# Attention and two feed-forward layers on one core: SBUF rooms taken in a fixed order, with moving and stationary operands 64 bytes apart modulo 256

## The chip, the cores and the metric

One core of a Trainium2 chip runs the whole kernel in one launch. The metric is the device time of one execution in microseconds; the time of the kernel before is the median of three runs.

## The reference

Sparse attention over 4 batches of 8 heads, 576 positions of 64 (four heads local, four strided by 32), gives x of 2304 x 512. Then two feed-forward layers without a residual follow, each from 512 to 2048 and back:

```python
def _moe_ref(x, w_in, w_out):
    h = x @ w_in
    g = np.where(h >= 1, h, np.where(h <= -1, 0.0, (h + 1) ** 2 / 4))
    return (g @ w_out).astype(np.float32)

def _moe2_ref(x, w_in, w_out, s, b):
    h = x @ w_in
    r = np.maximum(h, 0.0)
    g = s * (r * r) + b
    return (g @ w_out).astype(np.float32)
```

The output is `_moe2_ref(_moe_ref(x))`, all in float32. About nine tenths of TensorE's time are the four products with `w_in` and `w_out`.

## The kernel before

**Products.** Every float32 operand of the four big products is split into a high and a low part of type fp32r, and a product is three matmuls: high by high, high by low, low by high. Tokens go in 9 blocks of 256 (`g` from 0 to 8 for the first feed-forward layer, 9 to 17 for the second, called the first and the second half here); the 2048 hidden columns go in 8 pairs of two tiles of 128 (`p`). The step of one block and one pair has two layers:

- layer one (`layer1`, L838): the moving tile is a part of x (`xh` or `xl`, 256 columns), the stationary tile 128 columns of `w_in`; 2 x 4 x 3 = 24 matmuls go into the PSUM tile h;
- layer two of the first half (`layer2`, L993): the moving tile is a part of the activated g, the stationary one 128 columns of `w_out`; 24 matmuls into y;
- layer two of the second half (`layer2_fast`, L906): seven products of half-size blocks in place of eight (sums and differences of blocks are formed first, by `combine` at L881 for the activations and `w_combine` at L714 for the weights); here the *weights* move (256 columns) and g's parts (`gh`, `gl`) stand; 7 x 3 = 21 matmuls into y.

Each matmul loads its own stationary tile first; in the profile this is an LDWEIGHTS on PEld, which runs beside the matmul before it. Layer two of a pair comes `LAG = 2` pairs after layer one, so the rows of h and y alternate. Attention's small matmuls stand between them in about the first 345 us, and idle matmuls of a tile of zeros (`u`, both operands) fill gaps in the first 45 us.

**Order of work.** All operations are recorded by `Order` (L120), put into one order for all engines by `Order.issue` (L272) from prices and due times that are written in the kernel, and emitted there (L386, the line of nearly every row in the profile). Addresses play no part in that order, and neither the order nor any price is touched by the change.

**Rooms in SBUF.** A room is a tag with a shape; tiles of one tag use it one after the other. `Order.real` (L161) asks the pool for a room when the first tile of the tag is emitted, and rooms lie one behind the other in the order in which they were asked for, each start rounded up to 32 bytes. In the kernel before that is the order of first use. Most rooms are multiples of 256 bytes long, so the start modulo 256 changes only behind a room that is not: `half` (4 bytes), `narrow` (620 bytes) and `sbt` (8 bytes). This leaves, in the kernel before:

| rooms | start modulo 256 |
|---|---|
| xh, xl (moving in layer one) | 32 |
| w tiles of 4 KB, named w(f)_(0: w_in, 1: w_out), f from 0 to 15 | 32, but for these: 64 for w9_1 and w3_1; 128 for w7_1 and w9_0; 160 for w8_0, w7_0, w15_0, w15_1 |
| g (moving in layer two of the first half, gh in the second) | 64 |
| as, raw0, raw1 (gl in the second half) | 128, 160, 160 |
| xr1 (its four quarters hold weights in the second half) | 128 |
| u (zeros, both operands of the idle matmuls) | 128 |

All slices of these rooms that a big matmul reads start at a multiple of 256 bytes from the room's start, so the start modulo 256 is that of every slice. Pair p of the first half reads w tiles 2p and 2p + 1, the first with its 12 matmuls ahead of the other's in layer one, and in turns of three matmuls in layer two. In the stretch from 340 to 400 us of the profile, layer one has pairs 4 to 7 of block 5, 0 to 3 of block 6 and 0, 1 and on of block 7, and layer two runs two pairs behind: its pieces are pairs 2, 3, 4, ... of block 5 and then 0, 1, 2, 3 of block 6. The second half's weights take rooms that the first half's left free.

Of the kernel before, what the change touches and what calls it, by code (L numbers as in the profile page):

```python
# [20 lines left out]
P = 128  # L21
# [5 lines left out]
NF = DFF // P  # L27
# [89 lines left out]
    )  # L117


class Order:  # L120


# [30 lines left out]
    def bank(self, pool, choices, name, kind):  # L153


        t = self.tile(pool, [P, 512], F32, f"bank_{kind}", len(self.choices) + 1, name)
        self.choices[t.tensor.name] = choices
        self.uses[t.tensor.name] = []
        return t

    def real(self, x):  # L161

        if not isinstance(x, bass.AP) or x.tensor.name not in self.place:
            return x
        (tag, _), pool, shape, dtype, bufs, name = self.place[x.tensor.name]
        if x.tensor.name not in self.tiles:
            if self.in_psum(x):
                tag, bufs = self.taken[x.tensor.name], 1
            self.tiles[x.tensor.name] = pool.tile(shape, dtype, tag=tag, bufs=bufs, name=name)
        t = self.tiles[x.tensor.name]  # L170
        v = bass.AP(tensor=t.tensor, offset=x.offset, ap=[list(d) for d in x.ap])
        return v if x.dtype == dtype else v.bitcast(x.dtype)
# [217 lines left out]
def attention_moe_moe(ctx, tc, q, k, v, w1_in, w1_out, w2_in, w2_out, s_in, b_in, consts, out):  # L390
    nc = Order(tc.nc)
# [4 lines left out]
    ident = nc.tile(sb, [P, P], F32, "ident")  # L396
    narrow = nc.tile(sb, [P, N_CONST], BF16, "narrow")
    mask_l, mask_s, ident_b = narrow[:, :N_MASK_L], narrow[:, N_MASK_L:N_MASK_L + N_MASK_S], narrow[:, N_MASK_L + N_MASK_S:]
    sbt = nc.tile(sb, [P, 2], F32, "sbt")
# [287 lines left out]
    wc = {}  # L687
# [189 lines left out]
    def turn(i, rooms, name):  # L877
        n_room[i] += 1
        return rooms[n_room[i] % len(rooms)](name)

    def combine(g, p, u, h, gt):  # L881

        (a21, a11, a22, a12), (h21, h11, h22, h12) = [[x[:, i * P:(i + 1) * P] for i in range(4)] for x in (u, h)]
        s4 = turn(0, (main["qk"][0], main["v"][0]), f"s{g}_{p}")[:, :4 * P]
        s1, s2, s3, s4_ = [s4[:, i * P:(i + 1) * P] for i in range(4)]
        gh = gt.rearrange("p x n -> p (x n)")[:, :7 * P]
        if (g, p) == LAST:
            gl = xs[g, 1][1].rearrange("p x n -> p (x n)")[:, :7 * P]
        else:
            gl = turn(1, (*main["raw"], main["s"]), f"gl{g}_{p}")[:, :7 * P].bitcast(F32R)  # L890

        def split(x, c, eng=nc.gpsimd):
            nc.scalar.activation(out=gh[:, c], in_=x, func=AF.Copy)
            eng.tensor_tensor(out=gl[:, c], in0=x, in1=gh[:, c].bitcast(F32), op=ALU.subtract)

        nc.vector.tensor_tensor(out=s1, in0=h21, in1=a22, op=ALU.add)
        nc.vector.tensor_tensor(out=s2, in0=s1, in1=h11, op=ALU.subtract)
        nc.vector.tensor_tensor(out=s3, in0=h11, in1=a21, op=ALU.subtract)
        nc.vector.tensor_tensor(out=s4_, in0=h12, in1=s2, op=ALU.subtract)
        split(u[:, P:], slice(0, 3 * P))  # L900
        split(s4, slice(3 * P, 7 * P), nc.vector if g == LAST[0] and p >= NP - 2 else nc.gpsimd)
        gs[g, p] = gh, gl
# [48 lines left out]
    def last_two(g, p0, part):  # L951
        y, o = ys.pop(g), [turn(2, (main["qk"][1], main["v"][1]), f"o{g}_{p0}_{i}")[:, :DM] for i in range(2)]
        (c21, c22), (c11, c12), (p21, p22), (p11, p12), (m1, m6), (m2, m5), (m4, m7), (m3, _) = [
            (x[:, :HM], x[:, HM:]) for x in (*o, part[:, 0], part[:, 1], *y)
        ]
        pairs = [(p, gs.pop((g, p))) for p in (NP - 2, NP - 1)]

        def multiply(n, p, x):
            a, b = PRODUCTS[n]
            o, c, w = y[n // 2][:, n % 2 * HM:(n % 2 + 1) * HM], slice(a * P, a * P + P), wt[1, p][b]  # L960
            for i, j in ((0, 0), (0, 1), (1, 0)):
                nc.tensor.matmul(o, x[i][:, c], w[:, j], start=False, stop=p == NP - 1 and i == 1, skip_group_check=True)

        def leave(i, j, c, queue):
            r0 = (g - NBLK) * N + i * P
            queue.dma_start(out=out[r0:r0 + P, j * HM:(j + 1) * HM], in_=c)

        nc.in_line = True
        for i, n in ((0, 0), (0, 1), (0, 2), (0, 3), (1, 0), (1, 1), (1, 2), (1, 3), (0, 4), (0, 5), (1, 4), (1, 5), (0, 6), (1, 6)):
            multiply(n, *pairs[i])  # L970
        nc.in_line = False
        add = dict(op=ALU.add)
        nc.scalar.activation(out=c11, in_=m1, func=AF.Copy)
        nc.gpsimd.tensor_tensor(out=p11, in0=c11, in1=p11, **add)
        nc.vector.tensor_tensor(out=c21, in0=m6, in1=c11, **add)
        nc.gpsimd.tensor_tensor(out=p21, in0=c21, in1=p21, **add)
        nc.vector.tensor_tensor(out=c22, in0=m5, in1=c21, **add)
        nc.gpsimd.tensor_tensor(out=p22, in0=c22, in1=p22, **add)
        nc.vector.tensor_tensor(out=c11, in0=m2, in1=p11, **add)
        leave(1, 0, c11, nc.sync)  # L980
        nc.vector.tensor_tensor(out=p12, in0=c22, in1=p12, **add)
        nc.scalar.activation(out=p11, in_=m7, func=AF.Copy)
        nc.vector.tensor_tensor(out=p21, in0=m7, in1=p21, **add)
        nc.gpsimd.tensor_tensor(out=c22, in0=p11, in1=p22, **add)
        leave(0, 1, c22, nc.sync)
        nc.vector.tensor_tensor(out=c21, in0=p21, in1=m4, op=ALU.subtract)
        leave(0, 0, c21, nc.scalar)
        nc.vector.tensor_tensor(out=c12, in0=m3, in1=p12, **add)
        leave(1, 1, c12, nc.scalar)
# [36 lines left out]
    half = nc.tile(sb, [P, 1], F32, "half")  # L1026

    def room(tag, width):
# [4 lines left out]
        p=[room("qp0", 5 * P), room("qp1", S)], v=[room("v0", 9 * D), room("v1", 9 * D)],  # L1033
# [64 lines left out]
    with tc.manual_schedule():  # L1098
        nc.now = -100
        nc.sync.dma_start(out=ident, in_=consts[:, N_MASK_L + N_MASK_S:])  # L1100
        wide = x_room("wide", N_CONST)[:, 0]
        nc.sync.dma_start(out=wide[:, :N_CONST], in_=consts)
        nc.gpsimd.memset(half, 0.5)
        nc.vector.tensor_copy(narrow, wide[:, :N_CONST])

        nc.now = -1000
        zeros = nc.tile(sb, [P, 2 * N], F32R, "u", bufs=U_BUFS)
        nc.gpsimd.memset(zeros.bitcast(F32), 0.0)
        idle = nc.bank(ps, ("y1",), "idle", "y")
        nc.tensor.matmul(idle[:, :256], zeros[:, :P], zeros[:, :256], start=True, stop=True)  # L1110
        nc.fill(idle[:, :256], zeros[:, :P], zeros[:, :256])
        nc.now = -100
        for i, t in enumerate(STARTS):
            b, pair = divmod(i, 4)
            plan(Unit(b, FIRST_PAIRS[pair], borrowed(MEMORY[i]) if i in MEMORY else main, i < QUICK, i < NATURAL), t)
        for f in range(NF):
            plan_w(f)
        at(todo[0][0], pump)

        run(-1)  # L1120
        nc.sync.dma_start(out=sbt[:, 0:1], in_=bass.AP(tensor=s_in.tensor, offset=s_in.offset, ap=[[0, P], [1, 1]]))
        nc.sync.dma_start(out=sbt[:, 1:2], in_=bass.AP(tensor=b_in.tensor, offset=b_in.offset, ap=[[0, P], [1, 1]]))
        nc.now = -15
        x_split(0)
        nc.now = -2
        x_split(1)
        slot, behind = 0, []
        for n, (g, p0, p1) in enumerate(PASSES):

            order = []  # L1130
            for p in range(p0, p1):
                order.append((1, g, p0, p1, p))
                behind.append((2, g, p0, p1, p))
                if len(behind) > LAG:
                    order.append(behind.pop(0))
            nxt = PASSES[n + 1][0] if n + 1 < len(PASSES) else g
            if n + 1 == len(PASSES):
                order.insert(-2, order.pop(-2))
            for i, (layer, b, *pp, p) in enumerate(order):
                run(slot)  # L1140
                if slot == 0:
                    nc.fill()
                if layer == 1:
                    activate(b, p, layer1(b, p))
                else:
                    second(b, p, *pp)
                if i == p1 - p0 + 1 and nxt not in xs:
                    x_split(nxt)
                elif i == p1 - p0 + 1 and n + 1 == len(PASSES):
                    part = last_part(g, p0)  # L1150
                slot += 1
        nc.now += 1
        last_two(g, p0, part)
        nc.issue()


# [24 lines left out]
```

## Time and profile before

| | before |
|---|---|
| median of 3 runs | 897.74 us (897.33 to 898.22) |
| the profiled execution | 898.65 us |
| its span, first to last instruction | 896.9 us |
| mean granted TensorE clock | 0.998 of full speed |
| TensorE matmuls, weight loads | 8937 each, busy 99% and 98% |
| VectorE, ScalarE, GpSimd | busy 54%, 55%, 47% |
| DMA | 103.38 MB, 115 GB/s |

The profiled execution is one run with the profiler on; durations come from it. It is 0.9 us over the median. "h <- xh,w" names a matmul's result, its moving and its stationary tile, without buffer numbers.

### The profile page before, as it was taken

What the parts mean: (1) busy time and instruction counts of PE and PEld (TensorE: products, weight loads), DVE (VectorE), ACT (ScalarE), POOL (GpSimd) and SP (SyncE); (2) the same over time, 40 slices, a digit from 0 to 9 for tenths busy, and PEclk for the clock granted to TensorE, in tenths of its full rate; (3) what the DMA queues carried; (4) which work ended last, traced back from release to release, by engine and by line L of the source; (5) the groups of instructions that cost most, each with busy time, mean ns of one, the idle gap of its engine ahead of it and who ended that gap; (6) DMA issues with size and microseconds to landing.
All of it is one profiled execution on the core that took longest, in us unless ns stands there. A gap on an engine that the chain in (4) does not pass through costs nothing.

```text
span 896.9 us, 22117 instructions
## 1 busy us (share of the span) xinstructions
PE 888.9 (99%) x8937; PEld 877.1 (98%) x8937; DVE 483.4 (54%) x1006; ACT 489.9 (55%) x1086; POOL 423.6 (47%) x363
## 2 busy tenths in 40 slices
PE   9999999999999999999999999999999999999998
PEld 8999999999999999999999999999999999999998
DVE  3678764344334432333675778545457854454545
ACT  2577776444434442333644676656667655555554
POOL 6266562211121121223454578767755855544554
PEclk9999999999999999999999999999999999999999
DMA  9898523223312311003626633424334332222211
GB/s 176 235 284 276 191 75 98 66 47 78 66 21 64 73 66 48 25 24 102 212 88 211 206 125 133 150 94 147 137 104 180 118 117 94 96 96 94 95 48 48
DMA packets 125534, 103.38 MB, mean 115 GB/s; under 512 B 86688, under 2 KB 103840, under 8 KB 125432
## 3 DMA queue, kind: packets, MB, share of 16 engines
q1 hardware_dynamic: 122008, 100.52, 37.6%
q8 instruction: 70, 1.15, 0.5%
q10 hardware_dynamic: 2656, 0.85, 0.5%
q0 software_dynamic: 768, 0.60, 0.4%
q14 instruction: 32, 0.26, 0.1%
HBM read 73.63 MB, written 28.31 MB: 114 GB/s over the span
## 4 chain that ended last, share of the span: by engine, by line
PE 96%; ACT 1%; DVE 1%; POOL 1%; issue 0%; DMA 0%; SPq 0%; DVEq 0%; ACTq 0%; POOLq 0%
PE h L386 45%; PE y L386 42%; PE s L386 3%; PE idle L386 3%; PE o L386 2%; PE p L386 1%; PE t L386 1%; ACT u L386 0%; DVE wc L386 0%; ACT w L386 0%; DMA raw<-in_q_dram 0%; ACT g L386 0%; POOL g L386 0%; DVE u L386 0%; POOL xl L386 0%
## 5 line engine op out<-in xcount | busy, mean ns | idle before, releaser
L386 PE MATMUL h<-xh,w 128*128 128x256 f32 x2304 | 442.2, 284 | 0.5 <-ACT xh L386 0.3
L386 PEld LDWEIGHTS h<-xh,w 128*128 128x128 f32 x2304 | 368.4, 191 | 2.0 <-issue 0.6
L386 PE MATMUL h<-xl,w 128*128 128x256 f32 x1152 | 326.1, 283 | 0.0
L386 PE MATMUL y<-g,w 128*128 128x256 f32 x1728 | 222.1, 281 | 0.1
L386 PEld LDWEIGHTS h<-xl,w 128*128 128x128 f32 x1152 | 219.6, 191 | 0.1
L386 PEld LDWEIGHTS y<-g,w 128*128 128x128 f32 x1728 | 210.3, 188 | 1.0 <-DVE o L386 0.3
L386 POOL TENSOR_TENSOR g<-u,g 128x512 fp32r<-128x512 f32 x72 | 96.6, 1342 | 240.2 <-ACT g L386 158.8
L386 PE MATMUL y<-w,g 128*128 128x256 f32 x852 | 155.7, 281 | 0.0
L386 ACT ACTIVATE u<-h 128x512 f32<-128x512 f32 x144 | 85.8, 597 | 108.6 <-PE h L386 68.4
L386 DVE TENSOR_SCALAR u<-h 128x512 f32<-128x512 f32 x72 | 49.6, 690 | 152.3 <-PE h L386 152.2
L386 PEld LDWEIGHTS y<-w,g 128*128 128x128 f32 x852 | 130.9, 188 | 0.0
L386 ACT ACTIVATE u<-u,half 128x512 f32<-128x512 f32 x72 | 52.0, 723 | 126.0 <-DVE u L386 125.9
L386 POOL TENSOR_TENSOR gl<-u,g 128x384 fp32r<-128x384 f32 x71 | 74.1, 1044 | 97.3 <-ACT g L386 90.0
L386 PE MATMUL y<-w,gl 128*128 128x256 f32 x426 | 119.0, 281 | 0.0
L386 DVE TENSOR_SCALAR h<-h,sbt 128x512 f32<-128x512 f32 x72 | 58.8, 816 | 110.8 <-ACT h L386 110.7
L386 POOL TENSOR_TENSOR gl<-s,g 128x512 fp32r<-128x512 f32 x70 | 91.8, 1311 | 33.1 <-ACT g L386 30.1
L386 ACT ACTIVATE g<-u 128x512 fp32r<-128x512 f32 (+1 forms) x143 | 82.5, 578 | 32.9 <-DVE u L386 25.2
L386 POOL TENSOR_TENSOR w<-wc,w 128x512 fp32r<-128x512 f32 x56 | 77.1, 1379 | 39.4 <-ACT w L386 36.2
L386 PEld LDWEIGHTS y<-w,gl 128*128 128x128 f32 x426 | 80.1, 188 | 0.0
L386 DVE TENSOR_TENSOR u<-h,u 128x512 f32<-128x512 f32 x72 | 49.4, 686 | 28.8 <-ACT u L386 28.6
L386 ACT ACTIVATE g<-s 128x512 fp32r<-128x512 f32 x71 | 44.6, 629 | 20.8 <-DVE s L386 20.8
L386 DVE TENSOR_TENSOR s<-h,u 128x128 f32<-128x128 f32 x144 | 35.1, 284 | 32.6 <-ACT u L386 32.4
(112 smaller groups left out, 970.1 us busy)
## 6 DMA issues: line engine op xcount, KB each, us to landing
wr<-in_moe_w_in_dram SPq DMA_DIRECT2D x32, 512.0 KB
wr<-in_moe_w_out_dram SPq DMA_DIRECT2D x32, 512.0 KB
x<-o SPq DMA_DIRECT2D x36, 256.0 KB
scratch<-x SPq DMA_DIRECT2D x18, 512.0 KB
y<-o SPq DMA_DIRECT2D x22, 256.0 KB
scratch<-y SPq DMA_DIRECT2D x11, 512.0 KB
xhd<-xh SPq DMA_DIRECT2D x8, 512.0 KB
xld<-xl SPq DMA_DIRECT2D x8, 512.0 KB
```

Of the source, the lines that this page charges most:

```text
L386: getattr(getattr(self.nc, engine), op)(*args, **kw)
```

## The change

A list `HOMES` names every room of SBUF; `Order.settle` asks the pool for them in that order, after everything has been recorded and before `issue` emits the first instruction (L1154 before). `half` and `sbt`, each rounded up to 32 bytes, stand ahead of as, raw0, raw1 and narrow in the list, and narrow (620 bytes, 640 with rounding) ahead of xh, xl and g. `combine` puts gh 32 elements (128 bytes) further into its room.

```diff
--- before.py
+++ after.py
@@ -117,6 +117,13 @@
     )
 
 
+G_SHIFT = 32
+HOMES = (
+    "ident", "u", *(f"w{f}_{x}" for f in range(NF) for x in range(2)), "xr0", "xr1", "v0", "v1", "mx", "sm", "qp0", "qp1", "wc",
+    "half", "sbt", "as", "raw0", "raw1", "narrow", "xh", "xl", "g",
+)
+
+
 class Order:
 
 
@@ -157,6 +164,13 @@
         self.choices[t.tensor.name] = choices
         self.uses[t.tensor.name] = []
         return t
+
+    def settle(self, tags):
+
+        for tag in tags:
+            name = f"{tag}_0"
+            pool, shape, dtype, bufs, title = self.place[name][1:]
+            self.tiles[name] = pool.tile(shape, dtype, tag=tag, bufs=bufs, name=title)
 
     def real(self, x):
 
@@ -883,7 +897,7 @@
         (a21, a11, a22, a12), (h21, h11, h22, h12) = [[x[:, i * P:(i + 1) * P] for i in range(4)] for x in (u, h)]
         s4 = turn(0, (main["qk"][0], main["v"][0]), f"s{g}_{p}")[:, :4 * P]
         s1, s2, s3, s4_ = [s4[:, i * P:(i + 1) * P] for i in range(4)]
-        gh = gt.rearrange("p x n -> p (x n)")[:, :7 * P]
+        gh = gt.rearrange("p x n -> p (x n)")[:, G_SHIFT:G_SHIFT + 7 * P]
         if (g, p) == LAST:
             gl = xs[g, 1][1].rearrange("p x n -> p (x n)")[:, :7 * P]
         else:
@@ -1151,6 +1165,7 @@
                 slot += 1
         nc.now += 1
         last_two(g, p0, part)
+        nc.settle(HOMES)
         nc.issue()
```

The five engines' instructions and waits stand in the same order before and after. What is different is where the operands lie. After the change all w rooms, xr0, xr1, v, qp, wc and u start at 128 modulo 256, as, raw0 and raw1 at 192, xh, xl and g at 64, and gh, 128 bytes into g, at 192. The pairs of a matmul's moving tile and the next matmul's stationary tile, for the big products that follow each other directly, then stand as follows (difference: stationary minus moving, modulo 256; numbers of pairs):

| | before | after |
|---|---|---|
| layer one | 2310 at 0, 297 at 32, 203 at 96, 619 at 128 | 3342 at 64, 87 at 128 (switches to layer two of the second half) |
| layer two, first half | 1265 at 224, 215 at 0, 116 at 96, 105 at 64 | 1701 at 64 |
| layer two, second half | 754 at 32, 278 at 128, 157 at 96, 141 at 0, 139 at 192, 42 at others | 1418 at 64, 86 at 0 (switches to layer one), 7 at 192 (the last block) |

## Rows read from the trace of the kernel before

**Rows 1.** The page, part 1: busy us of each engine (share of the span) xinstructions.

```profile
PE 888.9 (99%) x8937; PEld 877.1 (98%) x8937; DVE 483.4 (54%) x1006; ACT 489.9 (55%) x1086; POOL 423.6 (47%) x363
```

**Rows 2.** The page, part 4: the chain that ended last, by engine and by line.

```profile
PE 96%; ACT 1%; DVE 1%; POOL 1%; issue 0%; DMA 0%; SPq 0%; DVEq 0%; ACTq 0%; POOLq 0%
PE h L386 45%; PE y L386 42%; PE s L386 3%; PE idle L386 3%; PE o L386 2%; PE p L386 1%; PE t L386 1%; ACT u L386 0%; DVE wc L386 0%; ACT w L386 0%; DMA raw<-in_q_dram 0%; ACT g L386 0%; POOL g L386 0%; DVE u L386 0%; POOL xl L386 0%
```

**Rows 3.** Groups by shape on PE: out<-in, rows*columns, shapes xcount, busy us, mean ns, idle.

```profile
L386 PE MATMUL h<-xh,w 128*128 128x256 f32 x2304 | 442.2, 284 | 0.5 <-ACT xh L386 0.3 <-DVE s L386 0.2
L386 PE MATMUL h<-xl,w 128*128 128x256 f32 x1152 | 326.1, 283 | 0.0
L386 PE MATMUL y<-g,w 128*128 128x256 f32 x1728 | 222.1, 281 | 0.1
L386 PE MATMUL y<-w,g 128*128 128x256 f32 x852 | 155.7, 281 | 0.0
L386 PE MATMUL y<-w,gl 128*128 128x256 f32 x426 | 119.0, 281 | 0.0
...
L386 PE MATMUL y<-halves,g 128*128 128x256 f32 x106 | 21.8, 281 | 0.9 <-ACT g L386 0.8
...
L386 PE MATMUL y<-halves,last_l 128*128 128x256 f32 x1 | 0.3, 279 | 0.0
```

**Rows 4.** Stretches: length, then PE, PEld, DVE, ACT, POOL busy (x), clock, DMA share, GB/s.

```profile
350.00:400.00 50.00, 50.00 (x425) 50.00 (x424) 15.46 (x24) 15.27 (x24) 11.35 (x9) 1.00 0.06 22
500.00:550.00 50.00, 49.75 (x417) 49.33 (x416) 42.69 (x88) 38.90 (x75) 35.40 (x28) 1.00 0.47 165
```

**Rows 5.** The chain, 340 to 400 us: start, us until the next piece, engine, tile, matmuls.

```profile
340.89 2.83 PE h L386 x24
343.73 2.83 PE y L386 x24
346.56 2.86 PE h L386 x24
349.42 2.81 PE y L386 x24
352.23 2.88 PE h L386 x24
...
392.05 2.87 PE h L386 x24
```

**Rows 6.** The chain, 590 to 640 us, second half of the work.

```profile
592.25 2.84 PE h L386 x24
595.09 2.47 PE y L386 x21
597.56 2.86 PE h L386 x24
600.42 2.48 PE y L386 x21
```

**Rows 7.** Groups by shape on PEld (weight loads), 352.3 to 354.9 us.

```profile
L386 PEld LDWEIGHTS h<-xh,w 128*128 128x128 f32 x15 | 2.4, 191 | 0.0
```

**Rows 8.** Groups by shape on PEld, 341 to 343.5 us.

```profile
L386 PEld LDWEIGHTS h<-xh,w 128*128 128x128 f32 x15 | 2.3, 188 | 0.0
```

**Rows 9.** Timeline of PE, 35 to 36 us: start, first start to last end, matmuls.

```profile
34.72 1.48 PE L386 MATMUL idle<-u 128*128 128x256 f32 x11
```

**Rows 10.** Timeline of PE, 395.98 to 396.06 us.

```profile
395.71 0.62 PE L386 MATMUL y<-g,w 128*128 128x256 f32 x4
```

**Rows 11.** Timeline of PE, 396.68 to 396.77 us.

```profile
396.40 0.64 PE L386 MATMUL y<-g,w 128*128 128x256 f32 x4
```

**Rows 12.** Stretches, matmuls into h alone: length, PE busy (x), clock, DMA share, GB/s.

```profile
0.00:50.00 50.00, 4.87 (x25) 0.98 1.04 221
50.00:100.00 50.00, 27.32 (x195) 0.99 0.93 285
```

**Rows 13.** Stretches, matmuls into y alone.

```profile
50.00:100.00 50.00, 20.60 (x157) 0.99 0.93 285
```

## The prediction

> **What bounds the kernel now.** First the page's busy times: TensorE is busy 99% of the 896.9 us span, its weight loads 98%, no other engine over 55% [rows 1]. Then the chain of work that ended last: 96% of it is TensorE, nearly all matmuls into h (layer one) and y (layer two) [rows 2]. So the time is a count of matmuls times their spacing. The groups by shape give the count [rows 3]: 2304 + 1152 for layer one, 1728 for layer two of the first half, 852 + 426 and eight smaller rows of 234 together for layer two of the second half. That is 3456 + 1728 + 1512 = 6696 matmuls of 256 columns, each with a weight load of its own. The mean of 281 to 284 ns in those rows is the length of one matmul in the pipeline, not the spacing; the reader should take the spacing from the chain, whose pieces follow each other start to start.
>
> In a stretch where TensorE never waits and the granted clock is 1.00 (2.4 GHz) [rows 4], the chain alternates between 24 matmuls into h and 24 into y [rows 5]. From the h piece at 340.89 to the h piece at 392.05 us lie nine pieces of each kind, 18 x 24 = 432 matmuls: 51.16 us / 432 = 118.4 ns. The y pieces of the second half have 21 matmuls in 2.47 or 2.48 us, 117.6 to 118.1 ns [rows 6]. 256 columns at 2.4 GHz are 106.7 ns. Some 12 ns of each spacing, 6696 x 11.8 = 79 us in all, are thus neither columns nor waits, and in that remainder lies everything this change can touch.
>
> **What the rows say about addresses.** The change alters only addresses. The question is whether the spacing hangs on (address of the stationary tile minus address of the moving tile) modulo 256, here called the difference; while one matmul streams, the weights of the next are read, so the pair is that matmul's moving tile and the next one's stationary tile. The old rooms are scattered enough to try this without a new run:
> - Difference 0, layer one, pairs whose two weight tiles both lie at 32 (10 and 11, 12 and 13): 2.86 and 2.88 us for 24 [rows 5], 119.2 and 120.0 ns. The idle matmuls, whose two operands are one tile, so also difference 0, show the same in another part: (1.48 - 0.28) / 10 = 120 ns [rows 9].
> - Difference 128 and 96, the same layer and the same moving rooms (weight tiles 8 and 9, at 340.89): 2.83 us [rows 5], 117.9 ns.
> - Difference 224, layer two (weight tiles 4 and 5, at 343.73): 2.83 us, 117.9 ns. Half 224 and half 64 (tiles 6 and 7, at 349.42): 2.81 us, 117.1 ns.
>
> The weight loads agree: 191 ns where the difference is 0 [rows 7], 188 ns at 96 and 128 in the same layer 11 us earlier [rows 8]. It is therefore not the layer, nor what other engines do: DMA share in this stretch is 0.06 and ACT and DVE are busy a third of it [rows 4].
>
> Difference 64 is rare before the change (weight tile 7 of layer two only, three matmuls at a time). Within one piece it takes two values. Four matmuls from 395.71 last 0.62 us; less the 0.28 of the last, three spacings of 113.3 ns [rows 10]. Four from 396.40, same tile and same difference, last 0.64: three of 120.0 ns [rows 11]. So the spacing depends on more than the pair at hand: on how far the two streams had fallen behind each other before. Difference 0 shows what a long stretch does: over ten idle matmuls the mean is 120 ns, the highest value of all, as if the streams settled at a fixed distance and stayed there. I take it that a long stretch of difference 64 settles too, and choose 113.3 for it, because no other difference in these rows comes that low and 120 is where difference 0 already sits. That is a choice between two values that the rows show, and the rivals price the other.
>
> **The change, part by part.**
> 1. *Order of work*: the instructions of all five engines stand in the same order, with the same waits. Nothing is added, removed or moved past a queue: 0 us.
> 2. *Differences*: with the new rooms layer one, layer two of the first half and the products of the second half all have 64, except where the second half switches between layers: there the last moving tile and the first stationary tile differ by 0 or 128, at 86 and 87 places. Price before: 6696 x 118.4 = 792.8 us (the second half's y pieces are a little under that, its h pieces at 2.84 to 2.86 a little over [rows 5, 6]). After, from below: 6696 x 113.3 = 758.7, a gain of 34.1 us. From above there are two bounds: the mean over both values of tile 7, which is the mixed piece's 117.1 less the 224 half's 117.9, so 2 x 117.1 - 117.9 = 116.3 ns: 778.7, a gain of 14.1; and the long value alone, 120.0: 803.5, a loss of 10.7. I take 113.3, for the reason above.
> 3. *Switches in the second half*: 173 places x three matmuls until the short spacing is back (the h piece at difference 0 is my guide only for the height, 120.0; three is an estimate) x 6.7 ns = 3.5 us given back.
> 4. *The first 100 us*: the DMA engines are full there (shares 1.04 and 0.93), so weights cannot arrive sooner. 25 + 195 matmuls into h and 157 into y [rows 12, 13] gain at most 377 x 5.1 = 1.9 us; I count it as lost to waits.
> 5. *The shift of g's part by 32 elements* (128 bytes): same writes and reads at another place in the same room, 0 us; the busy time of ACT, POOL and DVE has cover, since PE's lag of two pairs (about 11 us) stands between h and its use. If that cover is gone anywhere, it is at 500 to 550 us, where DVE is busy 42.7 and ACT 38.9 of 50 [rows 4]: 4.4% less time for the same work makes DVE 44.6 of 50 on that scale, still under PE.
> 6. *Attention's small matmuls and the tail after the last product*: their rooms move too, by no rule that a row here shows; with the idle matmuls they are about 10% of the chain [rows 2], some 90 us, and half a per cent of that is 0.4 us either way.
>
> Sum: -34.1 + 3.5 + 1.9 = -28.7 us. The profiled execution took 898.65 us (896.9 span and 1.75 around it), 0.9 over the median of 897.74, so the forecast is 897.74 - 28.7 = **869 us**.
>
> The Trainium skill speaks against the change. "TensorE: Matmul & The Clock Gate", Part 2, says that TensorE has two independent SBUF read ports and that loading the next weights takes no read bandwidth from the running matmul; "SBUF — State Buffer", in the section on the two sides, that PE's port never waits for anyone. By that rule addresses cost nothing and the sum is 0. The trace disagrees: 2.88 against 2.83 us for equal work [rows 5].
>
> **Rivals.**
> - *It settles in between* (chance 0.28). Runs of 64 keep alternating between 113 and 120 as tile 7 does: 14.1 gained, less half of items 3 and 4, 11.4: 886, with 875 to 889 as its span. For it: the alternation is what the rows show. Against it: in those rows difference 224 comes between, after the change nothing does.
> - *It settles at the long spacing* (0.10). The triple at 396.40 is the stable one. The turning point is a mean of 118.4 ns: above it the kernel is slower. At 120.0 it is 10.7 us more: 908; at 119, 902. For it: [rows 11]. Against it: no row shows 120 lasting at difference 64, and the piece as a whole is the shortest of its kind [rows 5].
> - *The address does not matter* (0.06), and the 2.83 and 2.88 come from the tiles' other properties (which banks of PSUM, what lies behind). Then 897.7. This is what the skill's rule would give. Against it: rows 7 and 8.
> - *The change doesn't do what it says*: excluded as far as it can be seen beforehand; the rooms as built have the differences given. *Another engine becomes the bound* would show first at 500 to 550 us: all of the gain of that stretch lost is 417 x 5.1 = 2.1 us, inside the range.
>
> **How the numbers follow.** Likeliest, 0.56: the short spacing, 864 (items 3 and 4 at nothing) to 874 (twice their price). With the next case it reaches to 889; 16 in 100 lie above. A spacing a little under 113.3 (0.62 is rounded: 112.0 would be 8.7 us more) takes the lower end to 858. A measurement of this kernel can tell about 0.2% (1.8 us). Faster by more: 0.56 + 0.28 = 0.84; within: 0.06; slower: 0.10.
>
> **What would show it.** Chain pieces of 24 matmuls into h and into y should both be about 2.72 us, with no difference between layers, and in 350 to 400 us over 440 matmuls should stand where 425 do. Weight loads of h should fall from 191 to 188 ns or less. PE should stay at 98% or more busy; waits of PE for ACT, DVE or DMA of several us would mean that the spacing fell and the time went elsewhere. If pieces of one kind stay at 2.86 or more while the differences are 64, the account by the difference is wrong. If they are near 2.79 and vary, the first rival holds.

## The result, and the profile after

| | before | changed |
|---|---|---|
| median, same chip (4 runs each) | 897.98 us (897.33 to 898.34) | 876.85 us (875.2 to 877.0) |
| ratio, 95% interval | | 0.9761 [0.9744, 0.9778] |
| profiled execution, its span | 898.65, 896.9 us | 876.75, 875.0 us |

The change gains 21.1 us, 2.4%; the forecast was a gain of 28.7 us, to 869. The page of the changed kernel, busy times and the chain that ended last, by engine and by line, stands against [rows 1, 2]:

```profile
PE 866.1 (99%) x8937; PEld 854.0 (98%) x8937; DVE 485.3 (55%) x1006; ACT 490.0 (56%) x1086; POOL 424.9 (49%) x363
...
PE 95%; ACT 1%; DVE 1%; DMA 1%; issue 1%; POOL 1%; POOLq 0%; DVEq 0%; ACTq 0%
```

The instruction counts are the same and no other engine was relieved: DVE, ACT and POOL are busy as long as before, PE 22.8 us less. PE is still 99% busy, so the time left the spacing of its matmuls. Stretches of the changed kernel (length, PE, PEld, DVE, ACT, POOL busy, clock, DMA share, GB/s):

```profile
350.00:400.00 50.00, 50.00 (x443) 50.00 (x443) 15.92 (x24) 15.27 (x24) 12.91 (x10) 1.00 0.06 22
500.00:550.00 50.00, 49.72 (x425) 49.31 (x424) 39.29 (x87) 37.56 (x72) 41.93 (x33) 1.00 0.38 136
```

At the same granted clock of 1.00, 443 matmuls stand where 425 did, and 425 where 417 did [rows 4]. The chain (start, us until the next piece, engine, tile, matmuls) shows where it came from. The stretch of [rows 5], which now starts 7.69 us earlier (the h piece of 340.89 is at 333.20):

```profile
333.20 2.72 PE h L400 x24
335.92 2.72 PE y L400 x24
```

All 20 pieces from 330.48 to 382.16 are 2.72 us: 113.3 ns, in both layers, whatever the weight tile. In the second half it looks different, where [rows 6] had 2.84 to 2.86 for h and 2.47, 2.48 for y:

```profile
740.92 2.74 PE h L400 x24
743.66 2.47 PE y L400 x21
746.13 2.74 PE h L400 x24
```

h is at 114.2 ns, but y still at 117.6: layer two of the second half gained nearly nothing, although its pairs stand at difference 64 like the rest. And before 305 us, where attention's small matmuls come between:

```profile
287.05 2.72 PE h L400 x24
289.77 1.64 PE s L400 x74
291.41 3.02 PE y L400 x24
294.44 2.83 PE h L400 x24
```

After the 74 small matmuls into s the same products at the same difference run at 2.83 us (117.9 ns) up to the next interruption, the small matmuls into p at 303.39 us. Worked out from the start times of all matmuls that follow each other directly: of 237 stretches of twelve spacings in the first half of the changed kernel, each begun at least eight matmuls behind an interruption, 194 have a mean of 113.3 ns (one of them 113.2), 43 one of 117.8, and none lies between. The mean spacings by part, before and after: layer one 119.2 and 114.6 (114.3 in the first half, 114.9 in the second); layer two of the first half 117.4 and 114.4; layer two of the second half 118.5 and 117.3; all together 118.6 and 115.2. The groups by shape on PE show it too (against [rows 3]; the mean is the length of one matmul, not the spacing):

```profile
L400 PE MATMUL h<-xh,w 128*128 128x256 f32 x2304 | 426.5, 279 | 1.1 <-DVE s L400 0.7 <-ACT xh L400 0.3
...
L400 PE MATMUL y<-g,w 128*128 128x256 f32 x1728 | 217.0, 279 | 0.1
L400 PE MATMUL y<-w,g 128*128 128x256 f32 x852 | 154.3, 281 | 0.0
...
L400 PE MATMUL y<-halves,g 128*128 128x256 f32 x106 | 22.1, 284 | 1.4 <-ACT g L400 1.0 <-DVE o L400 0.4
```

284 and 281 became 279 for h and the first half's y; the second half's y kept its 281. The weight loads of h between 333.2 and 335.9 us take 188 ns, where [rows 7] had 191:

```profile
L400 PEld LDWEIGHTS h<-xh,w 128*128 128x128 f32 x15 | 2.3, 188 | 0.0
```

### The profile page after: what moved, and what is told of

Read it like the earlier page. It is cut to its first block, busy times and chain, and to the rows that moved or that the text cites. A ratio compares the mean times of both kernels' runs of the same rounds, so it can differ in the third digit from the quotient of the medians.

```text
span 875.0 us, 22117 instructions
## 1 busy us (share of the span) xinstructions
PE 866.1 (99%) x8937; PEld 854.0 (98%) x8937; DVE 485.3 (55%) x1006; ACT 490.0 (56%) x1086; POOL 424.9 (49%) x363
## 4 chain that ended last, share of the span: by engine, by line
PE 95%; ACT 1%; DVE 1%; DMA 1%; issue 1%; POOL 1%; POOLq 0%; DVEq 0%; ACTq 0%
PE h L400 44%; PE y L400 41%; PE s L400 3%; PE idle L400 3%; PE o L400 2%; PE p L400 1%; PE t L400 1%; DMA wr<-in_moe_w_out_dram 1%; ACT u L400 0%; DVE wc L400 0%; ACT w L400 0%; DVE o L400 0%; DVE s L400 0%; ACT g L400 0%; POOL g L400 0%
## 5 line engine op out<-in xcount | busy, mean ns | idle before, releaser
L400 PE MATMUL h<-xh,w 128*128 128x256 f32 x2304 | 426.5, 279 | 1.1 <-DVE s L400 0.7
L400 PEld LDWEIGHTS h<-xh,w 128*128 128x128 f32 x2304 | 361.3, 189 | 2.7 <-issue 1.3
L400 PE MATMUL h<-xl,w 128*128 128x256 f32 x1152 | 320.7, 278 | 0.0
L400 PEld LDWEIGHTS h<-xl,w 128*128 128x128 f32 x1152 | 217.4, 189 | 0.1
L400 PE MATMUL y<-g,w 128*128 128x256 f32 x1728 | 217.0, 279 | 0.1
L400 PEld LDWEIGHTS y<-g,w 128*128 128x128 f32 x1728 | 205.3, 188 | 1.0 <-DVE o L400 0.3
L400 DVE TENSOR_SCALAR wc<-wr 128x512 int32<-128x512 int32 x64 | 49.5, 787 | 8.6 <-DMA wr<-in_moe_w_out_dram 6.6
```

The source lines that it names most:

```text
L400: getattr(getattr(self.nc, engine), op)(*args, **kw)
```

## The experiments

The theories, by the letters that the texts on record use. **A**: the difference alone sets the spacing of a long stretch. **B**: it is the absolute address, that operands now start at a multiple of 64 bytes. **C**: it is the fixed order, what lies beside what. **D**: a difference can have two steady spacings, and a stretch keeps one until something disturbs it. **E**: each pair's difference fixes its spacing, with no memory. **F**: the step of 128 at the entry to the second half's layer two puts it on the long spacing. **G**: those products are long of themselves. In what follows an order means the last nine names of `HOMES`; the changed kernel has half, sbt, as, raw0, raw1, narrow, xh, xl, g and `G_SHIFT` 32. The edits are shown by the names or lines that change; "..." stands for lines left out. Ratios are to the kernel before on the same chip (medians 897.85 to 898.97 us).

**1. e1_same: fixed order, difference 0 everywhere.**

```diff
-G_SHIFT = 32
+G_SHIFT = 0
-    "half", "sbt", "as", "raw0", "raw1", "narrow", "xh", "xl", "g",
+    "as", "raw0", "raw1", "xh", "xl", "g", "narrow", "half", "sbt",
```

> Fixed order of rooms, but every big room (w, x, g, as, raw) at the same start modulo 256 and gh not shifted, so that the difference (stationary minus moving, modulo 256) is 0 in all 6696 big matmuls. Theory A (the difference alone sets the spacing, and a long stretch settles at one value): 120 ns everywhere, pieces of 24 in 2.88 us and of 21 in 2.52 us, about 907 us, slower than both kernels. Theory B (what counts is that rooms start at a multiple of 64 bytes, which they still do): about 877 us. Theory C (what counts is the fixed order, which rooms are neighbours): about 877 us.

905.88 us, ratio 1.0086 [1.0061, 1.0112]: slower than before. Its chain, at 341 us and in the second half:

```profile
341.25 2.88 PE h L399 x24
344.13 2.88 PE y L399 x24
...
760.06 2.88 PE h L399 x24
762.94 2.52 PE y L399 x21
```

Every piece that nothing interrupts is at 120 ns, in both layers and halves. The rooms are in a fixed order and start at multiples of 64 bytes, as in the changed kernel, and the same instructions take 29 us more than there. A holds so far; B and C fall, and a fixed order is worth nothing by itself.

**2. e2_shift32: the changed kernel, all rooms 32 bytes further.**

```diff
-    "ident", "u",
+    "pad8", "ident", "u",
...
```

The lines left out have `settle` ask for the pad, 8 elements of 4 bytes.

> The changed kernel with a pad of 32 bytes ahead of all rooms: every address 32 bytes further, no room at a multiple of 64 any more, all differences as in the changed kernel. Theory A: no change, 876 to 878 us, pieces of 24 in 2.72 us in the first half. Theory B: the gain goes, 890 to 898 us. Theory C: 876 to 878 us.

876.06 us, ratio 0.9754 [0.9729, 0.9779]; not to be told from the changed kernel, and its chain at 331 us has the same 2.72:

```profile
333.66 2.72 PE h L402 x24
```

B falls a second time, now with the differences kept.

**3. e3_second192: 64 in layer one and the first half, 192 in the second half's layer two, 0 at all its switches.**

```diff
-G_SHIFT = 32
+G_SHIFT = 0
-    "half", "sbt", "as", "raw0", "raw1", "narrow", "xh", "xl", "g",
+    "half", "sbt", "narrow", "as", "raw0", "raw1", "xh", "xl", "g",
```

> The changed kernel, but gl's rooms and gh at 64 modulo 256 (gh not shifted, narrow ahead of as, raw0 and raw1): difference 64 in layer one and in the first half, 192 (minus 64) in layer two of the second half, and 0 at both switches of the second half. Theory A: layer one and the first half stay at 113.3 ns; layer two of the second half is at 117.3 ns in the changed kernel because the switch with difference 128 pushes it to a second, longer spacing. If 192 is as good as 64 and the switch with 0 does not push, its pieces of 21 fall from 2.46 to 2.38 us and the whole to about 869 us; if 192 has a spacing of its own near 117.5 the whole stays at 877; at 120 it is 881. Theories B and C: 877 us.

875.57 us, ratio 0.9751 [0.9728, 0.9774], the same as the changed kernel within the intervals. But the chain is another one:

```profile
742.41 2.47 PE y L399 x21
744.88 2.73 PE h L399 x24
747.62 2.38 PE y L399 x21
750.00 2.83 PE h L399 x24
752.83 2.47 PE y L399 x21
```

y takes 2.47 and 2.38 in turn, h 2.73 and 2.83 in turn. So layer two at 192 can run at 113.3, and layer one at 64 can run at 117.9. Going from h to y keeps the spacing, going from y to h changes it. That is D, and not E; A falls too, as far as it takes one spacing for each difference.

**4. e4_first192: 192 in layer one and the first half, 64 in the second half's layer two, 0 at its switches.**

```diff
-G_SHIFT = 32
+G_SHIFT = 0
-    "half", "sbt", "as", "raw0", "raw1", "narrow", "xh", "xl", "g",
+    "half", "sbt", "as", "raw0", "raw1", "xh", "xl", "g", "narrow",
```

> The mirror image: difference 192 in layer one and in the first half (x and g 64 bytes above the weights), 64 in layer two of the second half (gh not shifted), 0 at both switches of the second half. Theory A: layer two of the second half at 64 and without the switch of 128 settles at 113.3 ns, pieces of 21 in 2.38 us, 6 us gained there; layer one and the first half show what 192 is worth over long stretches: 113.3 would make it 871 us, 117.5 some 21 us more, 891, and 120 some 905. Theories B and C: 877 us.

886.56 us, ratio 0.9871 [0.9835, 0.9907]. The chain, at 340 us and in the second half:

```profile
340.12 2.83 PE h L399 x24
342.95 2.83 PE y L399 x24
...
751.40 2.40 PE y L399 x21
753.80 2.72 PE h L399 x24
756.52 2.48 PE y L399 x21
759.00 2.83 PE h L399 x24
761.82 2.39 PE y L399 x21
```

At 340 us everything is on the long spacing at 192. In the second half both layers alternate again, but now going from h to y changes the spacing and going from y to h keeps it, and the second half's y runs at 2.39 at difference 64, the very difference at which it takes 2.47 in the changed kernel. G falls: nothing in these products holds them at the long spacing.

**5. e5_homes_alone: the new order of rooms without the shift of gh.**

```diff
-G_SHIFT = 32
+G_SHIFT = 0
```

> The fixed order of rooms alone, gh not shifted: difference 64 in layer one and in the first half as in the changed kernel; in layer two of the second half 192 for the pairs that load gh and 64 for those that load gl; 0 at both switches of the second half. If layer two of the second half keeps whichever of the two spacings it comes in with (the switch with 0 did so in the mirror runs), its pieces of 21 are a mixture of 2.38 and 2.47 us and the whole is 873 to 877 us. If the mixed differences have a spacing of their own near 118, 878 us. If the shift of gh is what brings the gain: 890 us or more.

876.83 us, ratio 0.9765 [0.975, 0.978]. The second half alternates as in experiment 3 (y 2.38 and 2.50, h 2.83 and 2.73 from 744.25 us; 2.50 is 119.0 ns, somewhat over the long spacing, in pieces whose pairs stand at 64 and at 192). The shift brings nothing that can be measured: it turns "every y long, every h short" into "each in turn", with the same sum.

**6. e6_all192: 192 everywhere, the shift kept.**

```diff
-    "half", "sbt", "as", "raw0", "raw1", "narrow", "xh", "xl", "g",
+    "half", "sbt", "xh", "xl", "g", "narrow", "as", "raw0", "raw1",
```

> Difference 192 (minus 64) in all big products, with 128 and 0 at the switches of the second half, as the changed kernel has them with 64. If 192 is as good as 64 (two spacings, 113.3 and 117.8, and the way in decides which), about 877 to 888 us, and pieces of 24 in the first half are either 2.72 or 2.83 us and nothing between. If only 64 is good: 893 us or more, all pieces at 2.82 or over.

889.63 us, ratio 0.9909 [0.9889, 0.993]. The chain, in the first half and in the second:

```profile
219.35 1.47 PE s L399 x46
220.82 2.92 PE y L399 x24
223.74 2.72 PE h L399 x24
...
744.37 2.47 PE y L399 x21
746.84 2.83 PE h L399 x24
```

Most of the first half and all of the second is on the long spacing, but after some interruptions by attention, as here behind the 46 matmuls into s, the same products at the same difference take the short one. 64 and 192 have the same two spacings; they do not have the same share of each: by the count of stretches used above, 23 of 237 are at 113.3 here and 214 at 117.8.

**7. e7_flip: one spare matmul in the changed kernel, both operands one weight tile, in a stretch at 113.3.** It adds one product whose result is not used.

```diff
+                    if (b, p) == (5, 6):
+                        t = wt[0, 2 * p + 1, 0]
+                        spare = nc.bank(ps, U_BANKS, "spare", "u")
+                        nc.tensor.matmul(spare[:, :N], t[:, 0, :P], t[:, 0, :N], start=True, stop=True)
```

> The changed kernel with one matmul more, between layer one of block 5, pair 6, and the next layer two (about 344 us): both its operands are a weight tile, so the pair behind it has difference 0, every other pair keeps its own. Its result is not used. Theory D (two steady spacings at difference 64, 113.3 and 117.8 ns, kept until something disturbs it): the one disturbance moves the first half to 117.8 ns, pieces of 24 from 2.72 to 2.83 us from there to about 490 us, and costs some 5.7 us: 882 to 883 us. Theory E (the difference of the pair alone sets each spacing, without memory): 0.12 us for the one matmul, 877.0 us.

876.18 us, ratio 0.976 [0.9742, 0.9778]. Its chain:

```profile
346.35 0.12 PE spare L400
346.46 2.74 PE y L400 x24
349.21 2.72 PE h L400 x24
```

The flip that D expected did not come. About five matmuls are disturbed (0.02 us in the piece behind), then 113.3 is back. D in this form is too simple: this one wrong pair does not change the spacing of the stretch.

**8. e8_96_160: 96 in layer one and the first half, 160 in the second half's layer two.**

```diff
-G_SHIFT = 32
+G_SHIFT = 0
-    "half", "sbt", "as", "raw0", "raw1", "narrow", "xh", "xl", "g",
+    "half", "narrow", "as", "raw0", "raw1", "xh", "xl", "g", "sbt",
```

> Difference 96 in layer one and in the first half, 160 (minus 96) in layer two of the second half, 0 at the switches. The rows of the kernel before had 118.0 ns at 96 over 12 at a time and too few at 160. If every difference but 0 settles at one of the two spacings: 113.3 gives 868, 117.8 gives 896. If 96 keeps its own 118: about 895 to 898 us, like the kernel before.

894.66 us, ratio 0.9966 [0.9953, 0.9978]. Its chain:

```profile
304.66 2.85 PE h L399 x24
...
347.23 2.81 PE y L399 x24
350.04 2.82 PE h L399 x24
...
743.19 2.52 PE y L399 x21
```

96 gives 117 to 118 ns where nothing comes between, and up to 119 behind attention's small matmuls (2.85 at 304.66) and at every other h of the second half (2.82 and 2.85 in turn); 160 gives 120.0. Neither shows 113.3 over a long stretch.

**9. e9_bridge: one spare matmul at each entry to the second half's layer two,** both operands a weight tile, so that the two sides no longer step by 128 at once. Its results are not used.

```diff
+        t = wt[1, p]["t2"]
+        spare = nc.bank(ps, U_BANKS, "spare", "u")
+        nc.tensor.matmul(spare[:, :HM], t[:, 0, :P], t[:, 0, :HM], start=True, stop=True)
...
```

The lines left out have the spare matmul wait for what y's first one waits for.

> The changed kernel with one matmul more at each entry into layer two of the second half (72 of them; in 66 it stands right ahead of y's first): weights move and weights stand in it, so that the step from layer one has difference 64, 64 in place of 128. Its result is not used. Theory F (the step of 128 at the entry is what puts layer two of the second half on the longer spacing): most of its pieces of 21 fall from about 2.47 to 2.38 us, 4 to 6 us gained, against 72 x 0.113 = 8.2 us added: 878 to 882 us. Theory G (something in those products themselves makes 117.3 ns): pieces stay at 2.46 or more, 885 us.

883.3 us, ratio 0.9829 [0.9806, 0.9853]. Its chain:

```profile
622.77 0.12 PE spare L400
622.89 2.47 PE y L400 x21
```

y stays at 2.47 (53 of its 54 whole pieces at 2.47 or 2.48), so the spare matmuls are paid for and y gives nothing back. The 6.5 us over the changed kernel are fewer than the 8.2 that 72 of them cost; in the profiled executions most of the difference comes from around 650 us, where the changed kernel waits (see below) and this one does not. By the addresses of the rooms the spare matmul stands between h and y with 64 on both sides at 59 of the 72 places. F falls in this form.

**10. e10_first_part: the entry made 64 without a spare matmul.** The first of gh's seven parts lies 64 bytes lower than the others, so that most entries step by 64, with one pair at 0 after the first part.

```diff
-        gh = gt.rearrange("p x n -> p (x n)")[:, G_SHIFT:G_SHIFT + 7 * P]
+        gh = gt.rearrange("p x n -> p (x n)")[:, G_SHIFT - 16:G_SHIFT + 7 * P]
...
+            d = 16 * (c.start > 0)
+            h = gh[:, c.start + d:c.stop + d]
...
```

> The changed kernel with the first of gh's seven parts 64 bytes lower, so that the entry into layer two of the second half has 64 at 63 of 80 places; the price is one pair of difference 0 right behind it, and that part is written by instructions of its own on ACT and POOL. Theory F: if that pair of 0 is absorbed, as the single one in the first half was, the pieces of 21 fall to about 2.39 us and the whole to 870 to 872 us; if it sets the longer spacing as the step of 128 did, 877 us; ACT and POOL have time for the two instructions more.

876.35 us, ratio 0.9758 [0.973, 0.9785]. y is at 2.48 and h at 2.74 (from 620.25 us in its chain), as in the changed kernel:

```profile
620.25 2.48 PE y L400 x21
```

By itself this leaves it open whether the pair of 0 right behind the entry sets the long spacing, as the text above allows for. With experiment 9, which has no such pair, it is a second sign against F: the difference at the entry by itself does not decide.

**11. e11_shift_alone: the kernel before, with the shift of gh alone.**

```diff
-        gh = gt.rearrange("p x n -> p (x n)")[:, :7 * P]
+        gh = gt.rearrange("p x n -> p (x n)")[:, 32:32 + 7 * P]
```

> The other part of the change alone: the kernel before, its rooms as they were, with gh 32 elements further. The differences in layer two of the second half become 160, 128, 96 and 64 in place of 32, 128, 96 and 192, those elsewhere stay. The mirror run had 119.9 ns at a steady 160 against 118.5 at 32 before, over half of 1512 matmuls: 1 us slower, 898 to 900 us. If the shift carries a part of the gain by itself: below 895 us.

900.02 us, ratio 1.0015 [1.0004, 1.0027], some 1 us slower, as expected. Together with experiment 5: the rooms bring the whole gain.

**12. e12_three_steps: three spare matmuls in e6_all192, in a stretch on the long spacing,** with both operands a weight tile, then weight by x, then both x. Their results are not used.

```diff
+                    if (b, p) in ((5, 6), (6, 1), (7, 1)):
+                        t, x = wt[0, 2 * p + 1, 0][:, 0, :N], xs[b][0][:, 3]
+                        s, m = {5: (t, t), 6: (t, x), 7: (x, x)}[b]
+                        spare = nc.bank(ps, U_BANKS, "spare", "u")
+                        nc.tensor.matmul(spare[:, :N], s[:, :P], m, start=True, stop=True)
```

> The kernel with 192 everywhere, whose first half stands at 117.8 ns from about 341 us to its end near 490 us, with one matmul more at three places between layer one and layer two (results not used): at about 347 us with both operands a weight tile (difference 0 and 0 on the way), at 370 us with a weight tile and x (difference 192 throughout, a control), at 393 us with both operands x (0 on the way). If 113.3 and 117.8 ns are two steady spacings at one difference, a single disturbed matmul can move the stream from the one to the other: behind the first or the third the pieces of 24 go from 2.83 to 2.72 us and stay there, and the run is up to 5.4 us faster than the 889.6 us without them, although it does three matmuls more. The control changes nothing. If the long spacing belongs to this difference and stretch, or if neither disturbance moves it, all pieces stay at 2.83 and the run is 889.6 + 0.4 = 890.0 us.

892.29 us, ratio 0.9937 [0.9914, 0.996]. Its chain, around the first and the third spare matmul:

```profile
348.46 2.83 PE h L399 x24
351.29 0.13 PE spare L399
351.42 2.82 PE y L399 x24
...
391.10 0.12 PE spare L399
391.22 2.83 PE y L399 x24
```

None of the three takes the stretch off its long spacing; by the addresses of the rooms the first and the third bring one pair at 0 each. The 2.7 us over experiment 6 are more than the three matmuls (0.4 us). In the two profiled executions, 1.85 us apart, 1.5 us arise between 38 and 61 us: from 37 to 62 us the granted clock has a mean of 0.93 here, so a part of it is at 1.2 GHz, and of 1.00 in experiment 6. But the slowest of the four runs, 892.96 us, has a mean clock of 1.0, so what the rest of the 2.7 is stays open.

What the runs say of each difference over long stretches:

| difference | ns per matmul | where |
|---|---|---|
| 0 | 120.0 | e1_same, all parts |
| 64 | 113.3 or 117.8 | changed kernel; e3_second192 layer one; e4_first192 second y |
| 192 | 113.3 or 117.8 | e6_all192; e3_second192 second y; e4_first192 layer one |
| 96 | 117 to 118, up to 119 in some stretches | e8_96_160, layer one and the first half |
| 160 | 120.0 | e8_96_160, layer two of the second half |

## Why the prediction held, and where it missed

**The mechanism (the section on addresses, and item 2) was right.** The spacing hangs on the difference and not on the absolute address (e2_shift32), nor on the fixed order (e1_same), and 113.3, chosen from the three spacings of [rows 10], is a value to which a long stretch settles: pieces of 2.72, as forecast, in all 60 whole pieces of the first half behind 330 us. The price of 120.0 for difference 0, from the idle matmuls [rows 9], was also exact.

The choice of 113.3 had more behind it than [rows 10]: of the 33 undisturbed triples at 64 in layer two of the first half before, 16 have a mean of 113.3 ns or just over, and no triple at 0, 96 or 224 there is under 115.7. That it came out to the digit is in part luck, since [rows 10] are three spacings from times rounded to 0.01 us, 3 ns for each. And no row said which of the two values would last; the explanation given beside it, how far the two streams had fallen behind each other, is shown by no run.

**What failed is the assumption behind items 2 and 3, that a stretch at 64 has one value and that a switch only costs three matmuls until it is back.** 64 has two steady values. The text had seen that the spacing "depends on more than the pair at hand", and still took it that a long stretch settles to one. The higher one is not the 120.0 of [rows 11] but 117.8. The switches of the second half were priced at 3.5 us; in fact nearly every y piece of 21 stays on the long spacing from end to end (42 of 44 whole ones at 2.47). By the mean spacings that is (117.3 - 113.3) x 1501 = 6.0 us for y and (114.9 - 113.3) x 1675 = 2.7 for the second half's h, together 8.7, so 5.2 more than priced.

**A term was missing: the first half behind attention.** About a fifth of its matmuls, in stretches that begin after attention's small ones, run at the long spacing (2.83 at 294.44): (114.35 - 113.3) x 3379 directly following matmuls = 3.5 us. The step was to read 400 us of undisturbed products as if the 345 before them were the same.

**Item 4 was wrong the other way.** 1.9 us in the first 100 us were counted as lost to DMA; the same h piece at about 100 us starts 1.56 earlier than before (98.33 against 99.89), of which 0.73 stand at 10 us already, before any product, and so are not of this mechanism.

These three make 5.2 + 3.5 - 1.6 = 7.1 of the 7.6 us that are missing. Two smaller terms nearly cancel: the waits took 1.1 back (PE's idle time ahead of h went from 0.5 to 1.1 us and ahead of y<-halves,g from 0.9 to 1.4 [rows 3]), and the price before was too low, 118.4 where the mean of the whole trace is 118.6, which is 1.3 us more to gain. Most of the waits are at one new place: from 646.32 us on the chain of the changed kernel runs through a DMA of weights (6.79 us), ACT and DVE, and PE waits 0.8 us for DVE; the kernel before has no wait there.

**Items 1 and 5 held, and 6 nearly.** The counts of all engines are equal, the shift brings no gain (e5_homes_alone; alone, in the kernel before, it costs 1 us, e11_shift_alone), and no engine became the bound at 500 to 550 us, where DVE is now busy 39.3 of 50 and POOL 41.9. Of item 6, attention's small matmuls take the same time and the idle ones 0.7 us less, the 0.73 above.

**The rivals.** 876.85 lies outside the 864 to 874 of the likeliest case; the stated range holds it because the range takes in the next case. It lies in the span of that one, "it settles in between" (875 to 889), and the mean spacing, 115.2, is indeed between. But the picture of that rival, 113 and 120 in turn throughout, is not what happened: whole pieces take one of two values, and which one depends on the place. "It settles at the long spacing" is true of the second half's y alone, and of a spacing of 117.8, not 120. "The address does not matter" is refuted by e1_same: the same instructions in the same order take 905.9 us there and 876.9 here. That is also what the Trainium skill has to be measured against, "TensorE: Matmul & The Clock Gate", Part 2, by which the weight load takes no read bandwidth from the running matmul: read as the prediction reads it, that addresses cost nothing, it would make these two runs equal, and they lie 29 us apart.

**What stays open** is what chooses between the two spacings. Shown: attention's interruptions and the second half's switches choose anew; both layers and both differences can have either; a single spare matmul does not change it (e7_flip, e12_three_steps); changing the entry's difference alone does not free the second half's y (e9_bridge, e10_first_part). In the changed kernel the way into layer two ends at the long spacing nearly always, and the way out changes the spacing: behind a y on the long one h is short, behind a y on the short one h is long. With 0 at both switches one way keeps the spacing and the other changes it.

The trace of the changed kernel also shows y on the short spacing, in places that no experiment was built on. Where layer two is left for only one or two matmuls into h, the y piece behind them, of 15 to 21 matmuls, is at 113.3 to 114.7 ns, at all five such places (e2_shift32 and e7_flip have the same five). The chain of the changed kernel at two of them:

```profile
588.75 2.59 PE y L400 x22
591.34 0.12 PE h L400
591.47 2.29 PE y L400 x20
...
695.59 2.40 PE y L400 x21
697.99 2.84 PE h L400 x24
```

y goes from 117.7 ns to 114.5 across one matmul into h, and the h behind a short y takes 2.84. These entries step by 128 like all the others, so F falls here without any matmul added, and a disturbance of one matmul can move a stretch after all, when its pairs are those of both switches (0 and 128). That both operands move to other rooms at a switch may be what counts; it was only argued.

Two more things were not tried. To have 64 at both kinds of switch: the two layers' weights share rooms, so with g's parts anywhere one kind stays as it is. And 32, 128 or 224 over a whole kernel: 64 and 192 behave alike, and 96 (117 to 118) is close to what the kernel before had at 224 (117.9, [rows 5]), so no run here shows over a whole kernel that the period is 256 and not 128 bytes. The sign for 256 is weak: in layer one before, at most twelve in a row, 128 has a mean of 118.7 ns against 119.5 at 0. No version tried is measurably faster than the changed kernel; the second half's y, if all of it were short, would bring about the 6.0 us above (an estimate).

## What to carry to other kernels

When TensorE is busy all the time and its spacing lies above columns divided by clock, compare the pieces of the chain by the addresses of their operands before looking at any wait: here (stationary minus moving) modulo 256 set spacings from 113 to 120 ns per matmul, and two kernels that differ in addresses alone lie 29 us apart. Choose where rooms start and don't leave it to the order of first use, where a room of 4 bytes shifted all the rooms behind it; but a fixed order with the wrong difference was slower than none (e1_same). And where one row shows two values for the same case, price both as lasting, and ask for each stretch how it is entered.

## What the runs showed of the hardware that was not expected

- Two steady spacings at one and the same difference, 113.3 and 117.8 ns at 64 and at 192, kept over dozens of matmuls, with nothing lasting between them. Difference 0 has only one, 120.0 (e1_same).
- One spare matmul is absorbed within about five, at either spacing (e7_flip: 2.74 in place of 2.72 for the piece behind; e12_three_steps), while a switch of both operands to other rooms can move whole pieces from one to the other (e3_second192: y 2.47 and 2.38 in turn), even when it lasts for one matmul (changed kernel, y 117.7 and 114.5 at 588.75 and 591.47).
- The sign does not decide at 64 and 192, which have the same two values; 96 and 160, also opposite in sign, differ: 117 to 119 and 120 ns (e8_96_160; in different layers there, so the layer isn't ruled out for these two).
